# A new order of all tasks and a new choice of engines in a planned attention-then-SwiGLU kernel

## The chip, the cores and the metric

The kernel runs on one core of a Trainium2 chip. The metric is the device time of one execution in microseconds, lower is better. Five engines work side by side, each through its own instructions in order: PE (TensorE, matmuls; PEld is its weight load), DVE (VectorE), ACT (ScalarE), POOL (GpSimd) and SP (SyncE, which here only issues DMAs).

## The reference

A linear attention feeds a gated feed-forward layer.

```python
phi(x) = outer(S1 @ x, S2 @ x) per token and head      # 8 x 8 = 64 features
kv, z  = phi(k)^T v, sum over tokens of phi(k)         # per batch (4) and head (4); 1088 tokens, head size 32
attn   = (phi(q) @ kv) / (phi(q) @ z + 1e-6)
x      = attn as 4352 tokens x 128
xn     = x / sqrt(mean(x*x) + 1e-6) * rms_g
out    = (silu(xn @ w_gate) * (xn @ w_val)) @ w_out    # 128 -> 1536 -> 128
```

All of it is float32. The feed-forward products are made in three passes, each operand split into a rounded part and a rest (x_hi, x_lo, w_hi, w_lo): hi·hi + lo·hi + hi·lo.

## The kernel before

The tokens are cut into nine chunks (eight of 512, one of 256), the 1536 columns into twelve blocks of 128. A chunk with a block is a slot; there are 108. In a slot (`slot`, L783) PE makes the gate product g_ps (three passes, L802), then the value product v_ps (three passes, L802); ACT takes silu(g_ps) into s (L811); DVE multiplies h = v_ps·s (L814); ACT or DVE rounds h to h_hi (`rounded`, L348 to 351); DVE or POOL subtracts h_lo = h − h_hi (L832); and PE adds three passes of the down product to o_ps (L840). The last block goes in one exact pass (L821). There is one bank of PSUM for o_ps: when a chunk's sum is complete it is copied to SBUF by ACT or DVE (`copy`, L344 and L345, to o_sb or part; L857 where two parts are added), and only then can PE begin the next sum in it.

Around the slots stand, per batch, the keys (`kside`, L463: products with S1 and S2, the feature products phi, the sums kv) and, per chunk, the queries (`qside`, L572: features phiq, L651; numerator and denominator, L678; the division; root mean square, L709 and L721; the scaled xn, by ACT at L731 or by DVE at L724; x_hi, L764; x_lo, L767). From the third chunk on these go through DRAM by DMA. The weights (`weights`, L417) arrive as float64 in twelve loads w_raw (L422) and are joined to float32 (w_top, L401 or L404; w_full, L396) and split into w_hi (L350) and w_lo (L436). PE's filler matmuls on zeros (`keep_warm`, L382) stand where the plan sees PE without work at the start.

Nothing of this order is found at run time. The program makes a list of 1254 tasks (`Plan.add`, L162), each with the engines that may do it. Two tables then fix the program: `ORDER` (L53) is a permutation of the task numbers, and `ON` (L90) holds one letter for each task that has a choice (a for ACT, d for DVE, p for POOL). `follow` (L183) goes through `ORDER` with estimated durations and gives each task a start; `run` (L264) writes the instructions in order of these starts. So each engine's own order is fixed, and it waits at each instruction for the data and the buffer that this one needs.

```python
for t in self.tasks:
    t.on = {"a": "act", "d": "dve", "p": "pool"}[next(many)] if len(t.ways) > 1 else next(iter(t.ways))
for i in map(int, ORDER.split()):
    t = self.tasks[i]
    ...
    for d in t.deps:
        at = max(at, d.start if d.on == e == "pe" else d.end + self.hop(d.on, e))
```

DVE instructions with two SBUF inputs or in a fast mode, and all POOL instructions, are marked `lock` (`on_dve`, `on_pool`); `run` adds a dependency between such an instruction and the last one of the other engine ahead of it (`ties`, L277), so that they don't run at the same time.

Of the kernel before, what the change touches and what calls it, by code (L numbers as in the profile page):

```python
# [50 lines left out]
AHEAD_OF = (740, 1170)  # L51
HOP = {"act": 36, "dve": 34, "pool": 80, "pe": 54, "dma": 60}
ORDER = """  # L53
# [35 lines left out]
"""  # L89
ON = (  # L90
    "dapapadaddaadaadddaaaaapapdapapaadaadaadaapaadaadaadaadaddaadppddaapaadaaddadadadadadadadpdddaadddaaapapadadapapaadapapd"
    "dapapadapadapdpddddpadaaddadaapadaddpddadddadapadapddddadpadaadapaddpadapadddapapddadaaadpdaadpadadapddadddddapdpddddddd"
    "ddaaaapapapddapapdpdpddadaddpadadddaaaddddpapddadaddpadddapaddaddddaaddddpddapadadapadaddddpadpadddadadadadddapdda"
)
ATT = 3
QUARTERS = (1, 2, 3)
# [852 lines left out]
```

## Time and profile before

| what | us |
| --- | --- |
| median of 3 runs | 252.93 |
| the three runs | 252.86, 252.93, 254.64 |
| span of the profiled execution, first to last instruction | 250.3 |
| PE busy in the span | 246.4 (98%) |
| DVE, ACT, POOL busy | 180.5, 132.7, 81.9 |

The profile is of one execution. Its own device time is not listed; the span leaves out what lies before the first and behind the last instruction, and the median of the runs is 2.6 us above it. In rows of the timeline the first number is the start and the second the length, both in us; PE's matmuls overlap, so the time that one costs is the distance from its start to the next one's start, not its length.

### The profile page before, as it was taken

The numbers are of one execution on the slowest core, as the hardware profiler recorded it, in microseconds if no ns is written. First come the engines' busy times: TensorE is split into PE (matmuls) and PEld (weight loads), VectorE is DVE, ScalarE is ACT, GpSimd is POOL, SyncE is SP. The second block draws the span as 40 slices with busy tenths as digits, with TensorE's granted clock in tenths as the row PEclk, the third lists the DMA queues.
The fourth block names the chain that finished last, engine by engine and source line by source line (L and its number), as shares of the span: only waits on it lengthen the run. The fifth ranks groups of instructions, "written<-read, shape, count | busy, mean of one in ns | idle before, by whom it ended". The sixth has DMA issues, their size and how long they took to land.

```text
span 250.3 us, 5862 instructions
## 1 busy us (share of the span) xinstructions
PE 246.4 (98%) x2244; PEld 198.6 (79%) x2244; DVE 180.5 (72%) x410; ACT 132.7 (53%) x287; POOL 81.9 (33%) x80
## 2 busy tenths in 40 slices
PE   8999999999999999999999999999999999999995
PEld 5977788777888788878888788888888888888894
DVE  1899998799467887576587678855678576765672
ACT  3686998574444746353445643553256464355351
POOL 4447031343664223233550403265332203132201
PEclk9999999999999999999999999999999999999999
DMA  6979993542361332421510353251003001010010
GB/s 240 367 242 335 280 242 112 167 143 45 101 194 59 86 100 76 105 86 34 185 32 1 64 156 91 45 165 45 3 0 73 13 3 42 30 54 3 0 43 21
DMA packets 18539, 25.55 MB, mean 102 GB/s; under 512 B 3024, under 2 KB 9296, under 8 KB 18512
## 3 DMA queue, kind: packets, MB, share of 16 engines
q1 hardware_dynamic: 18080, 24.54, 32.9%
q10 hardware_dynamic: 432, 0.66, 0.7%
q8 instruction: 17, 0.28, 0.5%
q14 instruction: 10, 0.08, 0.1%
HBM read 20.40 MB, written 4.78 MB: 101 GB/s over the span
## 4 chain that ended last, share of the span: by engine, by line
PE 98%; DVE 0%; issue 0%
PE v_ps L802 29%; PE g_ps L802 29%; PE o_ps L840 28%; PE att L678 3%; PE att L531 2%; PE o_ps L382 2%; PE att L622 1%; PE o_ps L531 1%; PE att L594 1%; PE att L758 1%; PE att L497 1%; PE g_ps L678 0%; PE att L602 0%; PE v_ps L678 0%; PE att L821 0%; PE g_ps L519 0%
## 5 line engine op out<-in xcount | busy, mean ns | idle before, releaser
L811 ACT ACTIVATE s<-g_ps 128x512 f32<-128x512 f32 (+1 forms) x108 | 61.0, 574 | 71.0 <-PE g_ps L802 38.0
L814 DVE TENSOR_TENSOR h<-v_ps,s 128x512 f32<-128x512 f32 (+2 forms) x110 | 69.7, 646 | 39.9 <-PE v_ps L802 27.5
L832 POOL TENSOR_TENSOR h_lo<-h,h_hi 128x512 fp32r<-128x512 f32 (+1 forms) x42 | 52.9, 1267 | 104.3 <-DVE h_lo L832 43.8
L350 ACT CAST h_hi<-h 128x512 fp32r<-128x512 f32 (+1 forms) x70 | 41.3, 601 | 19.9 <-DVE h L814 17.4
L832 DVE TENSOR_TENSOR h_lo<-h,h_hi 128x512 fp32r<-128x512 f32 (+1 forms) x64 | 41.4, 651 | 5.5 <-ACT h_hi L350 3.6
L802 PE MATMUL v_ps<-x_hi,w_hi 128*128 128x512 f32 (+1 forms) x110 | 41.9, 381 | 0.0
L802 PE MATMUL g_ps<-x_hi,w_hi 128*128 128x512 f32 (+1 forms) x110 | 41.9, 381 | 0.0
L802 PE MATMUL v_ps<-x_hi,w_lo 128*128 128x512 f32 (+1 forms) x110 | 41.6, 378 | 0.0
L802 PE MATMUL g_ps<-x_hi,w_lo 128*128 128x512 f32 (+1 forms) x110 | 41.6, 378 | 0.0
L802 PE MATMUL g_ps<-x_lo,w_hi 128*128 128x512 f32 (+1 forms) x110 | 41.5, 379 | 0.0
L802 PE MATMUL v_ps<-x_lo,w_hi 128*128 128x512 f32 (+1 forms) x110 | 41.3, 378 | 0.0
L840 PE MATMUL o_ps<-h_hi,w_hi 128*128 128x512 f32 (+1 forms) x106 | 40.9, 386 | 0.0
L840 PE MATMUL o_ps<-h_hi,w_lo 128*128 128x512 f32 (+1 forms) x106 | 40.8, 385 | 0.0
L840 PE MATMUL o_ps<-h_lo,w_hi 128*128 128x512 f32 (+1 forms) x106 | 40.8, 385 | 0.0
L802 PEld LDWEIGHTS v_ps<-x_hi,w_hi 128*128 128x128 f32 x110 | 20.7, 188 | 5.0 <-DVE w_lo L436 0.5
L802 PEld LDWEIGHTS g_ps<-x_hi,w_hi 128*128 128x128 f32 x110 | 20.7, 188 | 4.5
L802 PEld LDWEIGHTS v_ps<-x_hi,w_lo 128*128 128x128 f32 x110 | 20.7, 188 | 4.3
L802 PEld LDWEIGHTS g_ps<-x_hi,w_lo 128*128 128x128 f32 x110 | 20.7, 188 | 4.3
L802 PEld LDWEIGHTS g_ps<-x_lo,w_hi 128*128 128x128 f32 x110 | 20.6, 188 | 4.1
L802 PEld LDWEIGHTS v_ps<-x_lo,w_hi 128*128 128x128 f32 x110 | 20.5, 188 | 4.1
L840 PEld LDWEIGHTS o_ps<-h_lo,w_hi 128*128 128x128 f32 x106 | 19.9, 188 | 4.3
L840 PEld LDWEIGHTS o_ps<-h_hi,w_hi 128*128 128x128 f32 x106 | 19.9, 188 | 4.2
(112 smaller groups left out, 246.4 us busy)
## 6 DMA issues: line engine op xcount, KB each, us to landing
w_raw<-w SPq DMA_DIRECT2D x12, 384.0 KB
bt<-far SPq DMA_DIRECT2D x24, 128.0 KB
at<-far SPq DMA_DIRECT2D x12, 256.0 KB
outT<-o_sb SPq DMA_DIRECT2D x8, 256.0 KB
q<-qT SPq DMA_DIRECT2D x7, 256.0 KB
turned<-xq SPq DMA_DIRECT2D x24, 64.0 KB
xt<-turned SPq DMA_DIRECT2D x6, 256.0 KB
vt<-v SPq DMA_DIRECT2D x4, 272.0 KB
```

Source lines behind the costliest of these rows:

```text
L350: "act": on_act(n, lambda: nc.scalar.copy(out=out(), in_=in_()), True),
L382: nc.tensor.matmul(out=warm[:1, :cols], lhsT=zeros[:, :1], rhs=zeros[:, :cols], start=True, stop=True)
L497: nc.tensor.matmul(out=pair[p]()[a * D:(a + 1) * D, :g], lhsT=sblk[p * HALF:(p + 1) * HALF, p * NB // 2:(p + 1) * NB // 2], rhs=kt()[p * H ...
L531: nc.tensor.matmul(out=kvv[r0:r0 + wide, h // 2, :], lhsT=phi()[:, t, h * F + f:h * F + f + wide], rhs=vt()[:, t, h, :], start=(t == 0 and ...
L594: nc.tensor.matmul(out=ab()[hf * HALF:(hf + 1) * HALF, t * HALF:(t + 1) * HALF], lhsT=q()[:, s1:s1 + HALF], rhs=sblk, start=True, stop=True,)
L622: nc.tensor.matmul(out=accs[p]()[a * D:(a + 1) * D, :m], lhsT=sab[rows, p].rearrange("p c o r -> p (c o r)"), rhs=q()[rows, a * m:(a + 1) ...
L678: nc.tensor.matmul(out=nv[n0:n0 + wide, t, p, :], lhsT=phi()[:, p, l0:l0 + wide], rhs=kvs[(s0 + l0) // S][:, p, :], start=True, stop=True,)
L802: nc.tensor.matmul(out=acc()[:, cs], lhsT=wt[:, j, i3, :], rhs=x()[:, cs], start=(i == 0), stop=(i == 2))
L811: act(n, lambda: nc.scalar.activation(out=s()[:, :n], in_=gps()[:, :n], func=AF.Silu), cols(gps, whole[0]), [s])
L814: cs.stop - cs.start, lambda cs=cs: nc.vector.tensor_tensor(out=h()[:, cs], in0=vps()[:, cs], in1=s()[:, cs], op=ALU.mult),
L832: eng.tensor_tensor(out=h_lo()[:, :n], in0=h()[:, :n], in1=h_hi().bitcast(F32)[:, :n], op=ALU.subtract)
L840: nc.tensor.matmul(out=o_ps()[:, :n], lhsT=wt[:, j, 2, :], rhs=x()[:, :n], start=first and i == 0, stop=last and i == 2,)
```

## The change

Both tables are replaced; nothing else is. `ORDER` is another permutation of the same 1254 numbers, `ON` another string of the same length. A line of each:

```diff
 ORDER = """
-1 0 2 6 9 3 14 10 15 4 32 33 7 37 16 5 64 34 18 38 19 12 26 27 22 20 146 39 28 147 11 23 24 151 35 40 41 65 17 13 148 21 25 36 29 152 153 149 66 72
...
+1 0 2 6 3 14 15 16 18 19 20 9 32 10 7 22 33 34 37 64 26 4 8 38 146 11 27 39 28 151 12 23 13 35 40 17 72 41 73 152 24 65 243 36 147 148 5 21 153 25 29 74 75 31
...
 ON = (
-    "dapapadaddaadaadddaaaaapapdapapaadaadaadaapaadaadaadaadaddaadppddaapaadaaddadadadadadadadpdddaadddaaapapadadapapaadapapd"
...
+    "dapdpddapdaadaadadaaadapapadpadaadaadaadadpaadaapaapaadaddaapdppdaddadpaaadadadadadadadadddddaapdaadadadadadadapaadapd"
...
 )
```

The computation and the number of useful matmuls are the same. The table is two lines shorter, so a line Lnnn of the kernel before behind it is Lnnn−2 in the changed one. Counted over the program's rows, the choice of engines moves as follows: six of the feature products phiq of the queries from DVE to POOL (12 and 2 before, 6 and 8 now); two of the later key products phi from POOL to DVE; four chunks' xn from ACT (30 instructions before, 14 now) to DVE (1, now 5); two of the w_lo from DVE to POOL; two of the copies o_sb from ACT to DVE (3 and 3 before, 1 and 5 now); four copies of the keys' and queries' factors (both) from ACT to DVE. ACT has 20 instructions fewer, POOL 8 more, DVE as many as before.

In the rows below a number in a name counts the instructions in the order in which the plan writes them, that is by planned start, over all engines.

The first place is PE at the start of the program: the keys' and queries' first products (g_ps, v_ps and att from sblk with kt and q), the fillers (const-float32-0.0) and the first transposes (from ident). Before:

```order
L382 MATMUL o_ps_97<-const-float32-0.0 1x96
L519 MATMUL g_ps_124<-sblk,kt_106 64x64 x2
L382 MATMUL o_ps_97<-const-float32-0.0 1x32
L594 MATMUL att_130<-sblk,q_109 64x64 x4
L382 MATMUL o_ps_97<-const-float32-0.0 1x128
L594 MATMUL att_144<-sblk,q_109 64x64 x4
L519 MATMUL v_ps_151<-sblk,kt_106 64x64 x6
L519 MATMUL v_ps_162<-sblk,kt_106 64x64 x4
L519 MATMUL g_ps_170<-sblk,kt_106 64x64 x6
L594 MATMUL att_179<-sblk,q_113 64x64 x4
L594 MATMUL att_186<-sblk,q_113 64x64 x4
L602 MATMUL g_ps_193<-ident,at_149 128x128 x4
```

The same stretch of PE after the change:

```order
L380 MATMUL o_ps_97<-const-float32-0.0 1x96
L517 MATMUL g_ps_124<-sblk,kt_106 64x64 x2
L517 MATMUL v_ps_129<-sblk,kt_106 64x64 x6
L592 MATMUL att_140<-sblk,q_109 64x64 x4
L380 MATMUL o_ps_97<-const-float32-0.0 1x64
L517 MATMUL g_ps_150<-sblk,kt_106 64x64 x6
L592 MATMUL att_162<-sblk,q_109 64x64 x4
L517 MATMUL v_ps_167<-sblk,kt_106 64x64 x4
L592 MATMUL att_176<-sblk,q_113 64x64 x4
L592 MATMUL att_183<-sblk,q_113 64x64 x4
L600 MATMUL g_ps_191<-ident,at_160 128x128 x4
```

Two groups of key products, each of six pairs (twelve matmuls in the trace), stand ahead of the second product with q instead of behind it, and two fillers have become one.

At the same place SP issues the loads, of the values (vt), of q and of the keys (kt) for the next batches, and of the weights (w_raw). Before:

```order
L482 DMA vt_115<-v 128x544
L422 DMA w_raw_118<-w 128x1536
L482 DMA vt_115<-v 128x272
L422 DMA w_raw_127<-w 128x1536
L570 DMA q_160<-qT 128x512
L570 DMA q_198<-qT 128x512
L471 DMA kt_207<-kT 128x640
L471 DMA kt_207<-kT 128x512
L422 DMA w_raw_237<-w 128x1536
L422 DMA w_raw_251<-w 128x1536
```

And now, from the last load of the first two chunks' q on:

```order
L568 DMA q_113<-qT 128x512
L480 DMA vt_115<-v 128x544
L480 DMA vt_115<-v 128x408
L480 DMA vt_115<-v 128x272
L420 DMA w_raw_122<-w 128x1536
L420 DMA w_raw_127<-w 128x1536
L568 DMA q_174<-qT 128x512
L469 DMA kt_189<-kT 128x640
L568 DMA q_199<-qT 128x512
L469 DMA kt_189<-kT 128x512
L469 DMA kt_220<-kT 128x512
L420 DMA w_raw_236<-w 128x1536
```

The first weights have gone behind the last piece of the values, and the third behind one more load of keys.

The second place is DVE in the same stretch, from the first feature products (at, phi) to the copy kv that the first numerators wait for. Before:

```order
L452 TENSOR_TENSOR at_149<-att_130,both_141 128x512
L452 TENSOR_TENSOR at_149<-att_144,both_158 128x512
L452 TENSOR_TENSOR phi_138<-v_ps_162,both_177 128x512
L452 TENSOR_TENSOR phi_138<-g_ps_170,both_200 128x768
L345 COPY phiq_210<-v_ps_202 128x2x256
L452 TENSOR_TENSOR at_219<-att_186,both_221 128x512
L396 SCALAR_TENSOR_TENSOR w_full_262<-w_raw_118,w_top_85 128x384
L556 COPY kv_73<-o_ps_212 64x2x33
```

After the change:

```order
L343 COPY both_145<-v_ps_129 128x192
L450 TENSOR_TENSOR at_160<-att_140,both_148 128x512
L450 TENSOR_TENSOR at_160<-att_162,both_172 128x512
L343 COPY both_197<-g_ps_150 128x192
L343 COPY both_206<-att_183 128x128
L450 TENSOR_TENSOR phi_138<-g_ps_150,both_197 128x768
L343 COPY both_234<-att_176 128x128
L450 TENSOR_TENSOR at_218<-att_176,both_234 128x512
L394 SCALAR_TENSOR_TENSOR w_full_255<-w_raw_122,w_top_85 128x384
L349 CAST w_hi<-w_full_255 128x256
L554 COPY kv_73<-o_ps_210 64x2x33
```

DVE has four small copies, and ahead of kv a cast of the first weights, that ACT did before; two larger pieces have gone to POOL and ACT.

The third place is late in the program, where one chunk's sum o_ps is copied out and PE begins the next in the same bank (o_ps_2615 and then o_ps_2951 before; o_ps_2674 and then o_ps_2963 now). Before, the copy is ACT's:

```order
L350 CAST h_hi_2848<-h_2833 128x512
L731 ACTIVATE xn_2860<-x_2737,rstd_2850 128x4x32 x4
L811 ACTIVATE s_2876<-g_ps_2842 128x512
L811 ACTIVATE s_2883<-g_ps_2865 128x512
L731 ACTIVATE xn_2908<-x_2852,rstd_2899 128x4x32 x2
L344 COPY o_sb_2929<-o_ps_2615 128x512
L811 ACTIVATE s_2939<-g_ps_2925 128x512
```

Now the copy of such a sum is DVE's:

```order
L812 TENSOR_TENSOR h_2919<-v_ps_2881,s_2895 128x512
L812 TENSOR_TENSOR h_2933<-v_ps_2923,s_2843 128x512
L812 TENSOR_TENSOR h_2939<-v_ps_2929,s_2927 128x512
L349 CAST h_hi_2949<-h_2939 128x512
L343 COPY o_sb_2951<-o_ps_2674 128x512
L812 TENSOR_TENSOR h_2969<-v_ps_2943,s_2947 128x512
```

And this is what PE does around it now, up to the first matmul of the next sum:

```order
L800 MATMUL v_ps_2929<-x_lo_2761,w_hi 128x512
L800 MATMUL g_ps_2935<-x_hi_2712,w_hi 128x512
L800 MATMUL g_ps_2935<-x_hi_2712,w_lo 128x512
L800 MATMUL g_ps_2935<-x_lo_2761,w_hi 128x512
L800 MATMUL v_ps_2943<-x_hi_2712,w_hi 128x512
L800 MATMUL v_ps_2943<-x_hi_2712,w_lo 128x512
L800 MATMUL v_ps_2943<-x_lo_2761,w_hi 128x512
L800 MATMUL v_ps_2953<-x_hi_2712,w_hi 128x512
L800 MATMUL v_ps_2953<-x_hi_2712,w_lo 128x512
L800 MATMUL v_ps_2953<-x_lo_2761,w_hi 128x512
L838 MATMUL o_ps_2963<-h_hi_2867,w_hi 128x512
```

The copy now stands in DVE's queue behind a product and a cast that wait for the value product v_ps_2929, three groups of passes ahead of the first matmul that needs the bank.

## Rows read from the trace of the kernel before

**Rows 1.** The page: span, and busy time of each engine (part 1).

```profile
span 250.3 us, 5862 instructions
PE 246.4 (98%) x2244; PEld 198.6 (79%) x2244; DVE 180.5 (72%) x410; ACT 132.7 (53%) x287; POOL 81.9 (33%) x80
```

**Rows 2.** The chain that ended last: by engine (page), and one of its pieces.

```profile
PE 98%; DVE 0%; issue 0%
...
101.67 3.50 PE o_ps L840 x15
```

**Rows 3.** A stretch: busy us of PE, PEld, DVE, ACT, POOL; clock; DMA; GB/s.

```profile
28.00:246.00 218.00, 218.00 (x1835) 176.99 (x1822) 158.92 (x350) 114.17 (x237) 68.30 (x54) 1.00 0.28 78
```

**Rows 4.** Waits of PE's weight loads: total us, times, longest.

```profile
PEld att L758 <- ACT w_hi L350: 0.5, 1, 0.5
PEld v_ps L802 <- DVE w_lo L436: 0.5, 1, 0.5
PEld att L594 <- DMA q<-qT: 0.4, 1, 0.4
PEld att L758 <- ACT xn L731: 0.4, 1, 0.4
```

**Rows 5.** Timeline of PE, 4 to 12 us: start, length, what.

```profile
5.40 0.58 PE L382 MATMUL o_ps<-const-float32-0.0 128*1 128x128 f32 x2
5.93 0.45 PE L594 MATMUL att<-sblk,q 128*64 128x64 f32 x8
6.21 0.75 PE L519 MATMUL v_ps<-sblk,kt 128*64 128x64 f32 x20
6.80 0.52 PE L519 MATMUL g_ps<-sblk,kt 128*64 128x64 f32 x12
7.15 0.64 PE L594 MATMUL att<-sblk,q 128*64 128x64 f32 x16
7.71 0.66 PE L602 MATMUL g_ps<-ident,at 128*128 128x128 f32 x4
8.21 0.60 PE L602 MATMUL v_ps<-ident,at 128*128 128x128 f32 x4
8.74 0.24 PE L531 MATMUL o_ps<-vt,phi 128*64 128x34 f32 x1
...
10.96 0.66 PE L602 MATMUL att<-ident,at 128*128 128x128 f32 x4
11.55 0.69 PE L678 MATMUL g_ps<-kv,phiq 128*64 128x66 f32 x16
```

**Rows 6.** Timeline of DVE, 5 to 12 us.

```profile
6.73 0.69 DVE L452 TENSOR_TENSOR at<-att,both 128x512 f32<-128x512 f32 x1 [0.22 <-ACT both L344]
...
8.44 0.96 DVE L452 TENSOR_TENSOR phi<-g_ps,both 128x768 f32<-128x768 f32 x1 [0.39 <-ACT both L344]
...
11.06 0.22 DVE L556 COPY kv<-o_ps 64x66 f32<-64x66 f32 x1
```

**Rows 7.** Timeline of ACT: the first weights' top parts.

```profile
9.05 0.65 ACT L401 CAST w_top<-w_raw 128x384 f16<-128x384 bf16 x1
```

**Rows 8.** The stretch from 5 to 10 us, columns as in rows 3.

```profile
5.00:10.00 5.00, 5.00 (x118) 4.20 (x116) 3.58 (x6) 3.04 (x11) 3.17 (x3) 1.00 1.05 394
```

**Rows 9.** Groups by line: busy us, mean ns, then idle time before them.

```profile
L651 DVE TENSOR_TENSOR phiq<-at,bt 128x512 f32<-128x512 f32 (+1 forms) x12 | 7.6, 640 | 1.5 <-POOL h_lo L832 1.4
L651 POOL TENSOR_TENSOR phiq<-at,bt 128x512 f32<-128x512 f32 x2 | 2.6, 1292 | 8.9 <-DVE h_lo L832 5.9 <-DVE ms L709 3.0
L724 DVE TENSOR_TENSOR xn<-x,rstd 128x512 f32<-128x512 f32 x1 | 0.7, 694 | 0.2 <-POOL rstd L721 0.2
L345 DVE COPY o_sb<-o_ps 128x512 f32<-128x512 f32 x3 | 2.1, 692 | 1.2 <-PE o_ps L840 1.2
L731 ACT ACTIVATE xn<-x,rstd 128x128 f32<-128x128 f32 x30 | 9.7, 392 | 3.7 <-POOL rstd L721 3.5
```

**Rows 10.** Timeline: o_ps copied by ACT, and the next sum's first matmul.

```profile
191.78 0.59 ACT L344 COPY o_sb<-o_ps 128x512 f32<-128x512 f32 x1 [0.83 <-PE o_ps L840]
...
193.68 0.40 PE L840 MATMUL o_ps<-h_hi,w_hi 128*128 128x512 f32 x1
```

**Rows 11.** Timeline, 117 to 126 us: a value product's last pass, and DVE behind it.

```profile
117.93 0.69 DVE L814 TENSOR_TENSOR h<-v_ps,s 128x512 f32<-128x512 f32 x1 [0.65 <-PE v_ps L802]
118.54 0.74 DVE L767 SCALAR_TENSOR_TENSOR x_lo<-xt,gain_t,x_hi 128x512 fp32r<-128x512 f32 x1
...
122.83 0.69 DVE L814 TENSOR_TENSOR h<-v_ps,s 128x512 f32<-128x512 f32 x1 [0.29 <-PE v_ps L802]
...
125.84 0.43 DVE L351 CAST h_hi<-h 128x512 fp32r<-128x512 f32 x1 [0.23 <-POOL h_lo L832]
...
122.34 0.39 PE L802 MATMUL v_ps<-x_lo,w_hi 128*128 128x512 f32 x1
```

**Rows 12.** Waits of DVE for POOL, the two largest: total us, times, longest.

```profile
DVE h L814 <- POOL h_lo L832: 3.0, 3, 1.2
DVE h_hi L351 <- POOL h_lo L832: 2.5, 4, 1.5
```

More of the change, by code (lines that the diff above doesn't have):

```diff
@@ L53 @@
 ORDER = """
[35 rows of a table removed]
[33 rows of a table added]
 """
 ON = (
-    "dapapadaddaadaadddaaaaapapdapapaadaadaadaapaadaadaadaadaddaadppddaapaadaaddadadadadadadadpdddaadddaaapapadadapapaadapapd"
-    "dapapadapadapdpddddpadaaddadaapadaddpddadddadapadapddddadpadaadapaddpadapadddapapddadaaadpdaadpadadapddadddddapdpddddddd"
-    "ddaaaapapapddapapdpdpddadaddpadadddaaaddddpapddadaddpadddapaddaddddaaddddpddapadadapadaddddpadpadddadadadadddapdda"
+    "dapdpddapdaadaadadaaadapapadpadaadaadaadadpaadaapaapaadaddaapdppdaddadpaaadadadadadadadadddddaapdaadadadadadadapaadapd"
+    "dapapadapadadapdpaddddaaaaddaaadpdpadapdpddapapdpaddddpdaappaadadddadadadadadadapadadapddapdddadddpdpdpapdpaddpadadada"
+    "dadappadddpdpapddapadapapddadadaddaadddddaddpapapdpddddapddaddddpddappdadddpaddpapdpapddadddaddddddapapaddpadadadddada"
 )
```

66 rows, old and new, of the table ORDER are left out of this document.

## The prediction

> **What bounds the kernel now.** I read the page first, then the chain, then the stretches, then single waits. The page shows PE busy for 246.4 of 250.3 us, with DVE at 180.5, ACT at 132.7 and POOL at 81.9 [rows 1]. A busy PE alone proves little, since its matmuls overlap; so look at the chain and at the distances. The chain that ended last stands on PE for 98% [rows 2], and one piece of it shows the pace: fifteen passes in 3.50 us, 0.233 us each. From 28 to 246 us PE has no idle time at all [rows 3], and the waits of its weight loads are a few of half a microsecond, all at the start: for xn, for weights, for a load of q [rows 4]. So behind 28 us nothing that another engine does faster can show, because PE is already fed without a gap; a better order can win only in the first 28 us. In the same stretch a worse one can lose anywhere.
>
> The clock is 1.00 throughout, the upper level [rows 3, 8], and the useful matmuls are the same ones. The sum is therefore made on the profiled execution's span of 250.3 us; the 2.6 us between it and the median of 252.93 I keep as they are.
>
> **The start, term by term.** PE stands from 5.40 to 5.93 on a filler, until the second half of q has landed [rows 4, 5]. From there to the first transposes at 7.71 it does 1.78 us of work, among it 32 key products from 6.21 to 7.15, 0.029 us each [rows 5]. After the change 24 of the 32 stand ahead of the wait, where the fillers were: 24 × 0.029 = 0.70 us go from behind the wait, and the first transposes could begin at 7.0. What is late next is DVE: the second feature product ends at 6.73 + 0.69 = 7.42 [rows 6], and its release is the same copy behind the same load, so the second transposes run at about 7.5 instead of 8.21 [rows 5]. That leaves 0.71 us for the sums kv, which began at 8.74.
>
> They don't get all of it. The first numerators, at 11.55, wait for the copy kv, which ran on DVE at 11.06 [rows 5, 6]. Now the first weights' w_full and a cast stand ahead of it, and w_full waits for w_top, which ACT did from 9.05 to 9.70 [rows 7]. Its load is issued behind one more piece of v (128 × 272 floats, 0.14 MB): at 394 GB/s [rows 8] 0.35 us later, so w_top ends at 10.05, w_full (0.55) and the cast (about 0.4, as for the 512 columns of rows 11) end at 11.0 less two overlaps of 0.08, and kv starts at 10.84 instead of 11.06. The gain is between 0.22 us (the load decides) and 0.71 (it is early enough); I take 0.35, near the lower end, since the copy is what the numerators wait for. From there to the first slot the chain has the same pieces, so 0.35 is carried.
>
> **The middle.** The choice of engines takes about 5 us from ACT (16 of the 30 pieces of xn that are busy for 9.7 us), gives POOL some 8 more, mostly six phiq at 1.29 us, and takes those from DVE at 0.64, which gets four xn and two o_sb at 0.69 [rows 9]. None of the three comes near the span, and PE covers it all: cost nothing by itself. Without that cover each would count with its full length.
>
> What can count is how late a piece ends before PE needs it. Two kinds of place show it. Before, one chunk's o_ps is copied by 191.78 + 0.59 = 192.37, and PE begins the next sum at 193.68: 1.31 us to spare [rows 10]. After the change the copy is DVE's, behind h_2939 and a cast. Let G be the start of the gate product behind v_ps_2929. The last pass of a value product starts 0.23 before G and takes 0.39; DVE began its product 0.10 after such an end (122.34 + 0.39 = 122.73, then 122.83) [rows 11], so at G + 0.26. The next instruction starts 0.61 later (117.93 to 118.54), the copy some 0.35 behind the cast's start (0.43 less 0.08), and it lasts 0.69: it ends at G + 1.91. PE is there after three groups of 0.70, at G + 2.10. So 0.2 us remain, 0.1 after the hand-over. That is still no wait. The copies that DVE makes number five instead of three; PE, in order, stands with everything behind its first down pass if one is late, and the next gate product, silu and product on ACT and DVE stand with it.
>
> For how often it is late I have bounds only. Below: zero, as rows of one shape repeat closely. Above: DVE now waits for POOL up to 1.5 us at a time, 0.8 us in the mean of the seven waits shown [rows 12]; at five copies with 0.1 to spare that is at most 5 × 1.4 = 7 us. A gain here is excluded, because PE has no gap to give back [rows 3]. I take one such wait at half its chance, (0.8 − 0.1) / 2 = 0.35 us, as DVE was idle for a quarter of the span and most waits fall elsewhere.
>
> The end is the same in both orders: the last eight exact passes, two additions, two stores. Cost nothing.
>
> **Sum.** −0.35 at the start, +0.35 in the middle, 0 at the end: span 250.3, time 252.93 + 0.0, say 252.9.
>
> **A rule against the change.** In the trace DVE instructions wait for POOL's h_lo, 5.5 us in the two largest rows [rows 12]; the program asks for this by a dependency, so the trace doesn't tell what the hardware alone would do. The Trainium skill ("SBUF — State Buffer", section "Who interferes with whom") says that a VectorE instruction with two SBUF inputs and a GpSimd instruction that reads SBUF exclude each other, and that the second to come is blocked for the other's whole length. By that rule the phiq moved to POOL hold DVE longer, whatever the program asked; the trace agrees as far as it goes, with waits up to 1.5 us.
>
> **Rivals.** First, the start gives all it could and no hand-over is late: −0.71, so 252.2. For it: PE's distances are steady, and the key products fit where the fillers were. Against: the weights' load ahead of kv. Chance 0.2.
>
> Second, POOL holds DVE in front of thin hand-overs, and the kernel becomes slower. The mechanism is that of the third place: an h_lo or phiq on POOL, 1.29 us, begins just before DVE's instruction ahead of the copy of o_ps; DVE waits 1.2 (the longest for h in rows 12), the 0.1 to spare is used up, and PE stands for 1.1. At the start's gain of 0.35 it takes three such places before the kernel is over 1% (2.5 us) slower; with four it is 4 × 1.1 − 0.35 = +4.05, so 257.0. For it: eight more POOL instructions and two more of the copies on DVE. Against: instruction lengths repeat, so that an order planned without a wait mostly has none. Chance 0.1.
>
> Third, the loads. The third and fourth weights are now issued behind 256 KB more of keys, 0.26 MB at 394 GB/s = 0.67 us later [rows 8], and ACT stands in order in front of them. If they were barely in time before, PE waits 0.67 for each, and +1.34 − 0.35 gives 253.9. For it: DMA is full in that stretch, share 1.05 [rows 8]. Against: PE's waits name weights only for 0.5 us [rows 4]. Chance 0.15.
>
> That leaves 0.55 for the forecast, whose own range is −0.6 to +0.8. Faster by over 1% would need 2.5 us out of the first 28; fillers and named waits there are 0.5 + 0.5 + 0.4 + 0.4 [rows 4] and about half a microsecond of the filler at 5.40 [rows 5], so all of it would have to go: 0.02. Slower by over 1% has the second rival, 0.1. The rest, 0.88, is within 1%, about what a measurement of this kernel can tell from no change. The range of 252.2 to 254.4 holds the forecast, the first and the third rival, and leaves out the second.
>
> **What would show it.** Right: the sums kv begin at 8.0 to 8.5, the first numerators at about 11.2, the first x_hi product 0.35 earlier than before; PE then busy without gaps up to the end; w_full named before kv. Wrong in the start: the second transposes still at 8.2. Wrong in the middle: waits of PE's weight loads for DVE's copy of o_ps, for h_lo or for x_lo behind 28 us, each of half a microsecond or more, and a stretch from 28 us on in which PE is not busy throughout. If PE shows no such wait and the time is still over 254.4, my reading that PE's pace is fixed is wrong.

## The result, and the profile after

The changed kernel takes 254.19 us in the median of 22 executions (253.26 to 255.63), the kernel before 252.86 (252.14 to 254.77): a ratio of 1.0057, with a 95% interval of 1.0041 to 1.0073. It is 1.3 us slower. It stays within 1% and inside the range, but the forecast of no change was wrong.

The page of after, span and busy time [rows 1], and its chain by engine [rows 2]:

```profile
span 252.8 us, 5859 instructions
...
PE 247.2 (98%) x2242; PEld 198.0 (78%) x2242; DVE 181.6 (72%) x410; ACT 125.1 (50%) x267; POOL 88.2 (35%) x88
...
PE 82%; DVE 5%; DMA 5%; POOL 2%; issue 2%; ACT 1%; SPq 1%; DVEq 0%; POOLq 0%; ACTq 0%
```

Busy PE says nothing: 98% in both. The chain does: it stood on PE for 98% before, and now for 82%. The stretch of rows 3 shows that PE has lost its unbroken run, by 0.95 us:

```profile
28.00:246.00 218.00, 217.05 (x1846) 174.11 (x1842) 157.48 (x339) 105.09 (x216) 73.87 (x62) 1.00 0.27 76
```

The waits of PE's weight loads from 28 to 252 us, for other engines (of the four in rows 4 one lay behind 28 us, the one for w_lo at 55.57; the prediction had put all at the start):

```profile
PEld o_ps L838 <- DVE o_sb L343: 1.6, 2, 1.3
...
PEld v_ps L800 <- DVE h L812: 1.3, 4, 0.5
...
PEld o_ps L838 <- DVE o_sb L855: 0.4, 1, 0.4
```

The largest, 1.3 us near 145 us, is in the chain, and PE stood idle for 0.90 us of it:

```profile
138.44 0.58 SPq L644
...
139.06 0.44 SPq L743
...
139.55 1.09 SPq L743
...
140.69 4.00 DMA outT<-o_sb
...
144.78 0.70 DVE o_sb L343
...
145.53 1.68 PE o_ps L838 x6
```

DVE's copy of o_ps needs one of two o_sb buffers, and that one is still being stored: the store of the second chunk (task 411), which SP issued at 92.44 before, now stands behind DMAs of another chunk and is issued at 140.69.

The start went as forecast up to the sums kv. Timeline of PE, DVE and ACT [rows 5 to 7]:

```profile
7.43 0.60 PE L600 MATMUL v_ps<-ident,at 128*128 128x128 f32 x4
7.96 0.24 PE L529 MATMUL o_ps<-vt,phi 128*64 128x34 f32 x1
...
11.32 0.69 PE L676 MATMUL g_ps<-kv,phiq 128*64 128x66 f32 x16 [0.47 <-DVE kv L554]
...
10.16 0.56 DVE L394 SCALAR_TENSOR_TENSOR w_full<-w_raw,w_top 128x384 uint32<-128x384 uint32 x1 [0.52 <-ACT w_top L399]
10.75 0.29 DVE L349 CAST w_hi<-w_full 128x256 fp32r<-128x256 f32 x1
10.96 0.21 DVE L554 COPY kv<-o_ps 64x66 f32<-64x66 f32 x1
...
9.44 0.63 ACT L399 CAST w_top<-w_raw 128x384 f16<-128x384 bf16 x1 [0.78 <-DMA w_raw<-w]
```

The sums begin at 7.96 instead of 8.74, but the copy kv stands behind the weights, at 10.96; the first numerators come at 11.32 instead of 11.55, and the first product with x_hi at 16.61 instead of 16.69.

To see where the rest goes I take, for each of PE's tasks, its start less the usual distances from start to start of all tasks ahead of it: the time in which PE has not advanced. The usual distances are a choice, so the differences between columns count, to about 0.1 us, and not the figures by themselves. In us, by stretch, from one profile of each kernel (the last four are experiments below):

| stretch | before | after | after again (e9) | old start (e4) | buffers (e11) | both (e12) |
| --- | --- | --- | --- | --- | --- | --- |
| up to 28 | 7.82 | 7.61 | 8.19 | 7.71 | 7.57 | 7.37 |
| 28 to 135 | 1.85 | 2.82 | 3.02 | 2.84 | 2.53 | 2.54 |
| 135 to 146 | 0.38 | 1.45 | 0.38 | 0.37 | 0.40 | 0.38 |
| 146 to 246 | 0.35 | 0.90 | 0.74 | 0.81 | 0.59 | 0.64 |

Between 28 and 135 us the new order loses about 1 us that no single row explains, and this repeats within 0.2 us in the three profiles that have it with the old buffers. The 1.07 us more near 145 us do not repeat. And the second profile of the changed kernel has no gain at the start.

### The profile page after: what moved, and what is told of

Its sections match the earlier page's. It is cut to its first block, busy times and chain, and to the rows that moved or that the text cites. A ratio compares the mean times of both kernels' runs of the same rounds, so it can differ in the third digit from the quotient of the medians.

```text
span 252.8 us, 5859 instructions
## 1 busy us (share of the span) xinstructions
PE 247.2 (98%) x2242; PEld 198.0 (78%) x2242; DVE 181.6 (72%) x410; ACT 125.1 (50%) x267; POOL 88.2 (35%) x88
## 4 chain that ended last, share of the span: by engine, by line
PE 82%; DVE 5%; DMA 5%; POOL 2%; issue 2%; ACT 1%; SPq 1%; DVEq 0%; POOLq 0%; ACTq 0%
PE o_ps L838 26%; PE v_ps L800 25%; PE g_ps L800 24%; DMA w_raw<-w 2%; DVE h L812 2%; PE att L676 2%; DMA outT<-o_sb 2%; DMA kt<-kT 1%; PE att L529 1%; POOL h_lo L830 1%; PE att L620 1%; SPq L743 1%; PE att L756 1%; PE g_ps L676 1%; POOL phiq L649 1%
## 5 line engine op out<-in xcount | busy, mean ns | idle before, releaser
L830 POOL TENSOR_TENSOR h_lo<-h,h_hi 128x512 fp32r<-128x512 f32 (+1 forms) x43 | 53.8, 1257 | 82.7 <-DVE h_hi L349 29.0
L719 POOL TENSOR_TENSOR rstd<-ms,mhalf 128x4 f32<-128x4 f32 (+1 forms) x10 | 9.8, 980 | 40.4 <-DVE ms L707 40.4
```

What stands on the lines that cost most here:

```text
L719: nc.gpsimd.tensor_tensor(out=rstd()[:, us, 0], in0=ms()[:, us], in1=mhalf[:, us], op=ALU.pow)
L830: eng.tensor_tensor(out=h_lo()[:, :n], in0=h()[:, :n], in1=h_hi().bitcast(F32)[:, :n], op=ALU.subtract)
```

## The experiments

Medians of 12 executions where no number stands; the kernel before was run beside each group on the same chip (252.54 with e1 to e4, 252.80 with e5 to e8, 252.53 with e9 to e12, 252.48 with e13 to e15). Moves in `ORDER` were made by a few lines behind the tables; each diff shows the pairs that were moved. Differences in us are between medians of one group; the interval behind a ratio tells what the scatter leaves of them. Lines that an edit adds shift the line numbers behind it.

**e1: the store early.** Task 411 goes back to about 88 us.

```diff
+ORDER = ORDER.split()
+for i, side, j in (
+    ("411", "after", "524"),
+):
+    ORDER.remove(i)
+    ORDER.insert(ORDER.index(j) + (side == "after"), i)
+ORDER = " ".join(ORDER)
```

> One task is moved in the changed kernel's order: the output store of the second chunk, task 411, is issued on SP right behind task 524, near 88 us, where the changed kernel issues it at 140.69. In the profile of the changed kernel the copy into o_sb at 144.78 had waited 2.25 us for the landing of this store and PE 0.90 us for the copy; from 144.06 to 146 PE loses 1.07 us more than in the kernel before. Theory A (the late store holds the one copy): that stall is gone, and the time falls from 254.2 to about 253.2. Theory B (a crowded VectorE that waits for GpSimd costs PE a little in many places): the copy at 144.78 starts early, but VectorE is late elsewhere, and the time stays at 254.2 within 0.3. If the store, now among the loads of 88 us, holds up loads, PE shows new waits for DMA behind 88 us and the time rises above 254.5.

Measured (5 executions): 254.81, ratio 1.0088 (1.0059 to 1.0117). **e2: three o_sb**, 11 executions:

```diff
-        o_sb = sb("o_sb", [P, 512], 2)
+        o_sb = sb("o_sb", [P, 512], 3)
```

> The changed kernel with three o_sb buffers instead of two and the same order: every store stays where it is, and no copy into o_sb waits for the landing of the store of the chunk two before it. Theory A: as with the early store, about 253.2, and without the stall near 144.8; if other chunks' copies wait for stores too, up to 0.3 us less than that. Theory B: 254.2 within 0.3, the waits of PE for VectorE as they were.

Measured: 254.03, ratio 1.0040 (1.0015 to 1.0065). In both the stall near 145 us is gone, and in neither does the time come near 253.2. Theory A falls as the whole cause. e1 lies above 254.5, as in its third outcome, but its list of PE's waits behind 28 us names no DMA. In their profiles both lost more at the start instead, 8.33 and 8.99 us up to 28 in the sense of the table.

**e3 and e4: the change cut at 17 us.** The first 120 numbers of one table (with their engines), then the rest of the other.

```diff
+START = 120
+HEAD = set(ORDER.split()[:START])
+ORDER = ORDER.split()[:START] + [i for i in REST.split() if i not in HEAD]
```

> The first 120 tasks of the changed kernel's order with their engines, up to about 17 us, and then the order and engines of the kernel before. In the profiles the changed kernel is 0.2 us ahead at 28 us. If the whole loss lies behind the start (both theories): 252.7, 0.2 below the kernel before, up to 0.35 below as forecast. If the new start is itself what costs later (its loads or buffers reach into the middle): above 253.2.

> The first 120 tasks of the order before with their engines, up to about 17 us, and then the changed kernel's order and engines. If the loss lies behind the start: 254.4, the changed kernel's 254.2 and the 0.2 us that its start gains; the stall near 144.8 is there as in the changed kernel. If the new start is what costs: 253.0, like the kernel before.

Measured: e3 253.67, ratio 1.0035 (1.0015 to 1.0054); e4 253.80, ratio 1.0043 (1.0016 to 1.0071). e3 has its second outcome, above 253.2; e4 has neither of its two, it lies between them. Each half costs 1.1 to 1.3 us by itself. The start, which I had counted as a gain, is one of the two causes.

The trace of e3 shows where. PE's weight loads of sixteen products of q with sab, and those of the numerators behind them, kernel before, then e3:

```profile
13.22 0.18 PEld L622 LDWEIGHTS att<-q,sab 64*32 64x32 f32 x16 [0.17 <-issue]
13.60 0.55 PEld L678 LDWEIGHTS g_ps<-kv,phiq 128*64 128x64 f32 x16 [0.20 <-issue]
```

```profile
12.97 0.17 PEld L666 LDWEIGHTS att<-q,sab 64*32 64x32 f32 x15 [0.17 <-issue]
13.46 0.10 PEld L666 LDWEIGHTS att<-q,sab 64*32 64x32 f32 x1 [0.32 <-issue]
13.77 0.55 PEld L722 LDWEIGHTS g_ps<-kv,phiq 128*64 128x64 f32 x16 [0.20 <-issue]
```

The last of sixteen loads waits for nothing that the program asked for ("issue"). What can be missing is the instruction itself, and the DMA packets bear that out. The DMA view has a queue of its own for instructions, one packet of 0.02 MB at a time (columns: packets, MB, share of the 16 engines). From 9 to 11 us, before and then after:

```profile
q1 hardware_dynamic: 369, 0.73, 100.3%
q8 instruction: 1, 0.02, 3.2%
```

```profile
q1 hardware_dynamic: 372, 0.79, 101.9%
```

In after the packet begins at 11.00. One load that was put ahead of it is one of keys (task 132, 320 KB): SP issues it in front of the fourth q's load, at 6.63, instead of behind it, at 8.20.

**e5: the key load late**, in e3. **e6: also DVE's copy kv in front of the cast.**

```diff
+    ("132", "after", "427"),
+    ("30", "before", "75"),      # e6 only
```

> The new start with the rest of the kernel before (253.67 in its run), and one load moved on SP: the first key load of the second block, task 132 of 320 KB, behind the load of the fourth q, task 427, as in the kernel before, where the new start issues it in front. In the trace of the new start PE's first instruction fetch of the body begins at 11.2 us, behind the packets of this load, and PE stalls 0.52 us at 13.8 on issue; in the kernel before it begins at 9.75 and PE does not stall. Theory S (the fetch stands behind the key load): the fetch begins near 10 us, the stall on issue at 13 to 14 us falls to 0.15 or less, and the time to 253.1. Theory Q (the new start reads the third q at its landing, so that a late DMA engine reaches PE in full): the fetch may come earlier, but the time stays at 253.6 within 0.3.

> As the kernel with the late key load, and VectorE's key-value copy, task 30, moved in front of the cast of the first weights, task 75. In the new start PE's first numerators at 11.32 had waited 0.47 us for this copy at 10.96. Theory (the copy behind the weights eats the start's gain): the copy begins 0.2 us earlier and the time is 0.2 below that of the kernel with the late key load alone. If ScalarE's copy of the other half, which ends 0.1 to 0.2 us before, binds next, 0.1 or less.

Measured: e5 253.25, ratio 1.0008 (0.9984 to 1.0033), so 0.45 above the kernel before where e3 was 1.13, though the two intervals overlap; e6 253.12, ratio 1.0007 (0.9981 to 1.0032). The hold at 13 us is gone in both traces, but the packet of e5 begins at 10.86 and not near 10, so the key load's place is only part of what sets it. The step from e5 to e6, 0.13, is within the scatter.

**e7: more buffers in e4. e8: the early key load in the kernel before.**

```diff
-        s, h = sb("s", [P, 512], 2), sb("h", [P, 512], 4)
+        s, h = sb("s", [P, 512], 3), sb("h", [P, 512], 6)
```

(and three o_sb as in e2); for e8 the pair `("132", "after", "243")`.

> The old start with the changed kernel's rest (253.80 in its run), with three s buffers instead of two, six h instead of four and three o_sb instead of two; order and engines the same. In its trace PE is held by 0.1 to 0.2 us at some ten products where the kernel before runs through, and the chains behind them often go through a buffer that another engine frees just then. Theory H (thin hand-overs through rotating buffers): the time falls by 0.3 to 0.8, to 253.0 to 253.5. Theory P (VectorE stands behind GpSimd, 13.6 us of such waits between 28 and 246 us against 8.2 in the kernel before): the order on VectorE is the same and so are its waits; 253.8 within 0.3.

> The kernel before with one load moved on SP: task 132, 320 KB of keys, in front of the fourth q's load, task 427, as the changed kernel has it. Theory S: PE's first instruction fetch begins near 11 instead of 9.75 us, PE stalls on issue at 13 to 14 us by 0.3 to 1.0, and the time rises by that, to 253.0 to 253.5. Theory Q: no change, 252.6 within 0.2.

Measured: e7 253.54, ratio 1.0009 (0.9982 to 1.0035), 0.74 above the kernel before where e4 was 1.26; both of its outcomes allow 253.54, so e7 alone does not decide. e8 252.99, ratio 0.9990 (0.9963 to 1.0017): by its time no cost is shown. Its profile does have the hold:

```profile
13.11 0.17 PEld L629 LDWEIGHTS att<-q,sab 64*32 64x32 f32 x13 [0.17 <-issue]
14.10 0.14 PEld L629 LDWEIGHTS att<-q,sab 64*32 64x32 f32 x3 [0.83 <-issue]
```

All profiles together show the mechanism. The packet's begin and end are from the trace's packet records; the last column is the distance from the first of these loads to the numerators, less the 0.38 us that it has in the kernel before:

| key load | kernel | packet, us | PE held, us |
| --- | --- | --- | --- |
| behind | before | 9.75 to 10.78 | 0 |
| behind | e7, e13 | 10.26 to 11.30, 10.34 to 11.43 | 0, 0 |
| behind | e6, e4 | 10.60 to 11.53, 10.64 to 11.58 | 0, 0.13 |
| behind | e10, e12 | 10.67 to 11.63, 10.73 to 11.82 | 0.12, 0.04 |
| behind | e5, e15 | 10.86 to 11.91, 11.06 to 11.99 | 0, 0.56 |
| in front | e11, after | 10.84 to 11.81, 11.00 to 12.03 | 0, 0.21 |
| in front | e3, e14 | 11.18 to 12.11, 11.23 to 12.20 | 0.42, 0.41 |
| in front | e9, e8 | 11.68 to 12.64, 11.74 to 12.73 | 1.01, 0.95 |
| in front | e1, e2 | 11.75 to 12.68, 12.21 to 13.27 | 0.93, 0.55 |

With the load in front the packet begins at 11.45 in the mean of eight, with it behind at 10.55 in the mean of nine, and PE is held 0.56 and 0.09. Not all of this is the load's place: with the new start it is 11.41 (seven profiles) against 10.78 (five), and with the old start and the load behind 10.25 (four). The break falls at the same load in every held profile, the sixteenth with the new start and the fourteenth with the old; there this load runs 1.24 to 1.45 us behind the packet's end (e3: 12.11, then 13.46), and where PE is not held, 1.39 us or more. e2 reaches these loads late, at 14.09, the others at 12.66 to 13.43, so the latest packet holds it by 0.55 only.

The table has two limits. One and the same start, that of the changed kernel, has packets from 10.84 (e11) to 12.21 (e2), so one profile does not tell what the load's place is worth. And what the hold costs in time is less certain than the hold: of the pairs that differ in the load's place none has intervals that are apart, and e8 shows no cost.

**e9 to e12: both repairs in the whole changed kernel, beside it.** e10 has the pair `("132", "after", "427")`, e11 the buffers of e7, e12 both and the move of task 30.

> The changed kernel as it is, beside the next three and on their chip, since the kernel before differed by 0.3 us between the two chips so far. Expected 1.3 us above the kernel before, as in its first runs; on each theory the same.

> The changed kernel with task 132, the key load, behind task 427 on SP. Theory S (an instruction fetch queued behind this load stalls PE at 13 to 14 us): 0.5 to 0.7 below the changed kernel on this chip, as the new start alone went from 1.13 to 0.45 above the kernel before. If the fetch was luck: 0.2 or less below.

> The changed kernel with three s, six h and three o_sb buffers, order and engines the same. Theory H (thin hand-overs through rotating buffers, the store's among them): 0.5 below the changed kernel on this chip, as the old start with the changed rest went from 1.26 to 0.74 above the kernel before, and in its trace none of the holds of 0.1 to 0.2 us at products that wait for a freed bank. Theory P (VectorE behind GpSimd): no change within 0.2.

> The changed kernel with the late key load, the more buffers and VectorE's key-value copy in front of the cast of the first weights. If the two causes add up: 1.0 to 1.3 below the changed kernel, at most 0.3 above the kernel before. If they overlap or a third cause is as large: 0.5 to 0.8 below it.

| kernel | median, range (us) | ratio to before (95%) |
| --- | --- | --- |
| e9, as it is (6 executions) | 254.54, 253.49 to 255.29 | 1.0077 (1.0055 to 1.0099) |
| e10, key load late (6) | 253.65, 253.42 to 254.88 | 1.0056 (1.0036 to 1.0076) |
| e11, buffers | 253.20, 252.81 to 253.89 | 1.0021 (1.0003 to 1.0039) |
| e12, both | 252.73, 252.52 to 253.78 | 1.0015 (1.0002 to 1.0027) |

Apart from the two moves each engine's sequence is the changed kernel's, and of the 2.0 us that it loses on this chip 1.8 are back. The buffers give 1.3 (e9 to e11), with intervals that are apart. The load's place gives 0.9 by the medians (e9 to e10), but those intervals overlap; e12 has the move of task 30 as well, and its two moves give 0.5 beside the buffers, within the intervals too. e9 itself stood 2.0 above the kernel before where 1.3 was expected from its first 22 executions; counted from that 1.3, e10 gives 0.2, e11 0.7 and e12 1.1.

The table by stretch tells where this comes from. Behind 28 us after again (e9) has lost 1.56 us more than the kernel before, e4 1.44, e11 and e12 still 0.94 and 0.98: the buffers take back 0.5 to 0.6, and about 1.0 stays. The rest of the step from e9 to e11 lies ahead of 28 us, where the packet of e11 came at 10.84 without any move and that of e9 at 11.68. e12 hides its 0.98 behind a gain of 0.45 at the start. PE's waits of e12 from 28 to 252 us, the ones that answer to those of after:

```profile
PEld v_ps L808 <- DVE h L820: 0.6, 2, 0.4
...
PEld o_ps L846 <- DVE o_sb L863: 0.3, 1, 0.3
PEld o_ps L846 <- DVE o_sb L351: 0.3, 1, 0.3
```

The chain of e12 stands on PE for 98% again. How a buffer holds PE shows at 69 us. The timelines of after, then of e11: ACT's s, DVE's product h, which needs s and frees a v_ps bank, and PE's next pass into that bank:

```profile
66.34 0.60 ACT L809 ACTIVATE s<-g_ps 128x512 f32<-128x512 f32 x1 [1.96 <-PE o_ps L838]
...
66.97 0.69 DVE L812 TENSOR_TENSOR h<-v_ps,s 128x512 f32<-128x512 f32 x1 [0.73 <-ACT s L809]
...
68.68 0.69 DVE L812 TENSOR_TENSOR h<-v_ps,s 128x512 f32<-128x512 f32 x1
...
69.42 0.50 PE L800 MATMUL v_ps<-x_hi,w_hi 128*128 128x512 f32 x1
```

```profile
65.96 1.09 ACT L809 ACTIVATE s<-g_ps 128x512 f32<-128x512 f32 x2 [1.56 <-PE g_ps L800]
...
66.59 0.69 DVE L812 TENSOR_TENSOR h<-v_ps,s 128x512 f32<-128x512 f32 x1 [0.26 <-ACT s L809]
...
68.30 0.69 DVE L812 TENSOR_TENSOR h<-v_ps,s 128x512 f32<-128x512 f32 x1
...
69.30 0.39 PE L800 MATMUL v_ps<-x_hi,w_hi 128*128 128x512 f32 x1
```

After: ACT starts s at 66.34. The releaser named in brackets is PE, but PE's gate product had ended at 65.77; what ended at 66.24 is DVE's h from the s buffer that ACT needs. So DVE's chain runs 0.4 us later, its second h ends at 69.37, and PE goes on at 69.42, 0.22 late. With three s buffers ACT starts at 65.96 and the second h ends at 68.99, ahead of PE at 69.30. Apart from the 0.90 us near 145 us this is the largest of such holds; the lists of PE's waits behind 28 us name nine for other engines in after and e4, and five in e12.

**e13 to e15: the buffers in the kernel before; s and h alone in after; the repaired start with the old rest and the buffers.**

> The control: the kernel before with three s, six h and three o_sb buffers. Its trace shows no hold of PE through these buffers behind 28 us. If the buffers matter only where an order has thin hand-overs: no change, within 0.15 of the kernel before. If they help any order: 0.5 or more below it, and then they explain nothing of the difference.

> The changed kernel with three s and six h buffers, and two o_sb as it has. With three o_sb as well it came to 1.34 us below the changed kernel; with three o_sb alone it stood 1.49 above the kernel before, where the changed kernel stands 1.33 to 2.0 above. If the s and h buffers carry the gain: within 0.3 of the kernel with all three, 253.2 to 253.5. If the store's wait for o_sb does: 254 or more, with the wait near 144.6 in the trace.

> The new start with the late key load and the key-value copy in front of the cast, the rest of the kernel before, and the three more buffers: what each half does best. If what is left of the start's gain, 0.1 us at 28 us in the trace without the buffers, comes through: 0.1 to 0.3 below the kernel before. If the later instruction fetches decide, as in that kernel's trace, where one at 60.3 us held PE by 0.62: 0.3 above it.

Measured: e13 252.28, ratio 0.9986 (0.9967 to 1.0004): the control holds, the old order gets 0.2 by the medians, not clear of none, from buffers that give the new one 0.7 to 1.3. e14 253.73, ratio 1.0044 (1.0024 to 1.0065), between its two outcomes: s and h alone stand 1.25 above the kernel before, o_sb alone (e2) 1.49, all three (e11) 0.67. Its profile has the store's wait again:

```profile
144.27 0.69 DVE L343 COPY o_sb<-o_ps 128x512 f32<-128x512 f32 x1 [1.85 <-DMA outT<-o_sb]
...
145.01 0.50 PE L838 MATMUL o_ps<-h_hi,w_hi 128*128 128x512 f32 x1 [0.34 <-DVE o_sb L343]
```

e15 253.17 without one execution of 343.9, ratio 1.0023 (1.0003 to 1.0043): not faster. In its trace, as in e5 and e6, an instruction packet at 60.3 to 60.7 us, which the kernel before has at 56.8, holds PE for 0.6 to 0.9 us at 63, again at one and the same load, 1.35 to 1.41 us behind the packet's end: the same mechanism at another place. No version here is shown to beat the kernel before.

## Why the prediction was wrong

**The start up to the copy kv: right.** Forecast: second transposes at about 7.5, sums up to 0.71 earlier, the copy at 10.84, numerators 0.35 earlier within 0.22 to 0.71. Measured: 7.43, 0.78, 10.96, and 0.23. The reason given, w_full and the cast ahead of the copy, is what rows of DVE show. The 0.35 was a third too large.

**"From there to the first slot the chain has the same pieces, so 0.35 is carried": this step failed.** It counted the pieces that the rows list, and the instruction fetch is none of them. The fetch comes 1.2 us later with the new start (11.41 against 10.25 in the means), 0.6 of it by the key load's place; in after PE was there 0.2 us earlier, and so the gain can turn into a loss: the first product with x_hi came 0.08 us earlier in after and 0.60 later in e9. e3, the start alone, is 1.13 above the kernel before, and 0.45 with the key load moved back. The program's own plan does have an estimate for these fetches (`follow`, with FETCH in L111 and FETCH_AT in L113 of the kernel before), which I had not read; worked out with either table, it holds PE for none of them. The third rival had the right cause, keys issued ahead of other loads, and the wrong victim: it asked which weights come late, at 0.67 us each. The weights did not; the instructions did.

**The middle: the right kind of cause, the wrong count and partly the wrong place.** I took "one such wait at half its chance", 0.35 us, at DVE's copies of o_ps. The table shows about 1.4 us from 28 us on in e4, where the term had 0.35; the list of waits names nine there, four of them at value products that wait for DVE's h and three at o_ps. With more buffers 0.5 us of the 1.4 goes away; what the other 1.0 is made of beside the five waits that e12 still lists, no run shows. I had looked at one hand-over of the new order and concluded that 0.1 us to spare is still no wait. Where a hand-over has no slack, a few tenths of a microsecond by which an engine is late reach PE, as at 69 us, and there is no gap from which they come back. That sentence of mine, that PE has no gap to give back, was right and should have made the upper bound count for more.

**The store: not foreseen.** It falls on the copy that I named as thin, but what is late there is a DMA. In all five profiles with two o_sb and the late store, DVE's copy waits 1.0 to 2.3 us for it; PE is held between nothing and 1.07 us. The five show no simple order in this: the store landed 3.0 to 4.0 us after its issue, and with PE 0.9 us late from the fetch (e9) it landed in time. That the store's hold and the fetch's take turns, so that one repair alone shows little (e1, e2, e14), is a guess: e14 has both holds, e4 hardly either, and no run tested it.

**The second rival, POOL holding DVE: half of it came.** DVE's waits for POOL from 28 to 246 us grew from 10.9 to 21.8 us in sum (8.2 to 13.6 in the four largest rows, which the expectation of e7 gives). The three largest of after, for rows 12:

```profile
DVE h_lo L830 <- POOL h_lo L830: 5.1, 4, 1.5
DVE h_hi L349 <- POOL h_lo L830: 3.8, 3, 2.1
DVE h L812 <- POOL h_lo L830: 3.0, 4, 1.3
```

The rule that I weighed there ("SBUF — State Buffer", section "Who interferes with whom", of the Trainium skill) agrees with this growth, but the growth is no test of it, since the program asks for such waits itself. And e12 keeps 18.9 us of these waits and stands 0.2 above the kernel before: most of them cost PE little. The third of the rows, 3.0 us in front of h, is absent from e11 and e12, where h has six buffers: it was a wait for a buffer that POOL's h_lo still read, not for the shared access. The program has no `lock` on h (L814), so the same holds for the row of h in rows 12, which I had put down to that dependency.

**The end: right, but not what lies outside the span.** From PE's last instruction to the end of the span it is 3.0 us in both. The 2.6 us between span and median, which I kept as they are, did change: each listed execution of the kernel before and of e8 lies 2.1 to 2.2 us above its span, each of the changed kernel and of all others, e13 too, 1.7 to 1.9. So the changed kernel loses about 1.7 us in the span and gets 0.36 back outside it, e12 stands some 0.55 above the kernel before by the span, and the 0.2 that e13 gained is none by the span. No run shows what the 0.36 us are. And the profile of before was a quick one: its 250.3 stands for some 252.4, below the median.

What stays open: the 1.0 us behind 28 us that e12 still loses, the 0.36 us outside the span, what the fetch costs in the median, and which part of the buffers' gain is the store's.

## What to carry to other kernels

In a kernel whose main engine runs without a gap, a new order can only lose behind the start, and here it lost much of it in small holds, few of which stand out in the lists of waits; add up the engine's own lag by stretch in both traces, and try one more buffer before another order. Loads that an order issues early can stand in front of the instruction fetch too: look at the waits named "issue" and at the queue of instruction packets. And where each of two repairs shows little, run them together before you call either wait harmless; the control of the old order with the same repair belongs beside it.

## What was not expected of the hardware

The first instruction packet of PE in the body (0.02 MB) takes 0.9 to 1.1 us and begins later where more loads were issued ahead of it (11.41 against 10.78 us with the same start); where PE was held, it ran on 1.24 to 1.45 us after the packet's end; a hold of up to 1.0 us at 13 us followed in these runs, and of up to 0.9 at 63. The Trainium skill ("Runtime: NRT & Kernel Launch", section "Instruction fetch mechanics") says that the sequencer fetches the next block through its own DMA queue while the current one runs, and that the cost of crossing a block is mostly hidden. The queue of its own is in the trace; the cost was hidden in six of these seventeen profiles at this block altogether, and up to 1.0 us of it showed in the others. One store of 256 KB, beside the loads of another chunk, landed 3.0 to 4.0 us after its issue in five profiles, too wide a spread to plan a buffer on.
